# Weights of a gated feed-forward layer loaded and cast by GpSimd's queue at the start of the kernel

## The chip, the cores and the metric

One core of a Trainium2 chip runs the whole program. The metric is the device time of one execution in microseconds (us); lower is better. The profile is of one execution, taken by the hardware profiler; its span is the time from its first to its last recorded event.

## What is computed

Attention with decay over blocks of 64 positions, for 4 batches, 8 heads, 768 positions and a head size of 64, and then a gated ("highway") layer over the 3072 x 512 result:

```python
intra = np.einsum('bhic,bhjc->bhij', qb, kb) * Dmask[None]
intra = np.einsum('bhij,bhjd->bhid', intra, vb)
inter = np.einsum('bhid,bhde->bhie', qb * lam_pow[None], kv_state)
out[:, :, sl] = intra + inter
kv_state = lam_block * kv_state + np.einsum('bhsd,bhse->bhde', kb_dec, vb)
...
H = np.maximum(x @ w_h, 0.0)
T = 1.0 / (1.0 + np.exp(-(x @ w_t + b_t)))
return T * H + (1.0 - T) * x
```

q, k, v, the two 512 x 512 weights `w_h` and `w_t`, the bias and the output are float32.

## The kernel before

The kernel works on 12 chunks n of 256 positions, three to a batch. A chunk has two halves b of 128 positions. A name such as q0 or k1 means q of chunk 0, k of chunk 1. Nothing is scheduled by the machine: the string `PLAN` (L17 to L68) is a list of steps in the order in which they are written to the engines' queues, and every engine works through its own steps in that order. A step is a letter, the chunk and its parts, the engine behind @ and the PSUM banks behind =. The steps that matter here:

- `Lq`, `Lk`, `Lv` (function `load`, L214): loads of q, k and v, in f32, two of 256 KB for each chunk and tensor, all issued by SyncE (SP). There are five buffers of each kind (`BUFS`, L70), so the first five chunks' loads wait for nothing but their turn. One row in DRAM is 1 KB long for q (four positions of 64 floats) and 512 B for k and v.
- `CK`, `CQ`, `CV` (L230, L235, L242): casts of k, q and v to bf16, q and v with a multiplication by powers of lambda.
- `TK`, `TQ` (L255): transposes of k and q on TensorE; `EB` (L268) copies the result to SBUF as `kqT`.
- `S`, `SP`, `U`, `I`, `A` (L291 to L364): the matmuls of the scores, of the state, and of the output of the attention; `M` (L343) multiplies the scores with the mask `tri`, `KE` copies the state, `D` (L366) copies the output to SBUF as `xT`.
- `F` (L389): the matmuls of the feed-forward layer, x times w_h or w_t, with the bf16 weights `w_b`. `PB`, `G`, `H`, `X`, `AD`, `ST` are the bias, the sigmoid, the gating, the sum and the store.
- `W` (`load_w`, L223) and `WC` (`cast_w`, L227): loads and casts of the weights. SP issues four loads of 512 KB, `W.0.0`, `W.0.1`, `W.1.0`, `W.1.1` (weight, half of its rows), to the f32 buffers `w_f`; their rows in DRAM are 2 KB long. Eight casts of 128 x 512 copy them to `w_b`: five on ScalarE (ACT), two on VectorE (DVE), one on GpSimd (POOL). The first step that needs them is `F.0.0.0`.
- `Z` (`spin`, L421) and `ZT`: matmuls on a blank tile whose results are not used, which fill TensorE's waits, above all in the first 17 us.

Ahead of the plan stands the set-up (L123 to L169): ACT loads lambda and the bias and a table, POOL makes the identity, two lists of indices (iota, L135 and L137) and the mask `tri` (L139 to L142), and DVE and ACT make the powers of lambda. A copy or cast on ACT or DVE has the line of the helper `copy` (L110, L112); on POOL L112 too.

Of the kernel before, what the change touches and what calls it, by code (L numbers as in the profile page):

```python
# [16 lines left out]
PLAN = """  # L17
Lq.0.1 Lq.0.0 CQ.0.1@POOL CQ.0.0@POOL Lk.0.0 Lk.0.1 CK.0.0@DVE ZT Z.6=6 TQ.0.0=01 Lv.0.0 Lv.0.1 CK.0.1@ACT Lq.1.0
Lq.1.1 TK.0.0 EB.0.0@ACT EB.0.1@DVE Z.5=6 S.0.0=01 CV.0.1@DVE CV.0.0@DVE Z.3=6 U.0.0 B=2 Lk.1.0 Lk.1.1 Lv.1.0
KE.0.0@DVE CQ.1.0@POOL I.0.1=3 S.0.1=45 U.0.1 CK.1.1@POOL Lv.1.1 PT@ACT M.0.1.1@DVE CK.1.0@DVE M.0.0.1@DVE CQ.1.1@POOL  # L20
CV.1.0@POOL Lq.2.1 Lk.2.0 Lk.2.1 Lq.2.0 W.0.0 Z.5=6 TK.1.1=56 TQ.1.1 M.0.0.0@DVE EB.1.1@DVE CV.1.1@POOL M.0.1.0@DVE
EB.1.0@ACT W.0.1 KE.0.1@ACT BC@ACT Z.7=4 SP.1.0=561 KE.1.0@ACT M.1.1.1@DVE M.1.1.0@DVE Lv.2.1 Lv.2.0 A.0.1=2 A.0.0
I.1.1=0 I.1.0=4 SP.1.1=6 CK.2.2@POOL D.0.1@ACT D.0.0@ACT M.1.0.0@DVE M.1.0.1@DVE W.1.0 TK.2.1=35 W.1.1 KE.1.1@ACT
WC.0.0.1@ACT WC.0.0.0@DVE Lq.3.1 Lq.3.0 WC.0.1.1@DVE WC.0.1.0@ACT CQ.2.2@POOL XT.0=2 A.1.1 A.1.0 D.1.1@DVE TQ.2.1
D.1.0@ACT F.0.0.0=6 XE.0@DVE EB.2.0@ACT XT.1=0 F.1.1.0=2 CV.2.2@POOL WC.1.1.0@POOL EB.2.1@DVE XE.1@DVE PB.0.1@ACT=4
WC.1.0.1@ACT PB.0.0@ACT=1 H.1.1@DVE WC.1.0.0@ACT F.0.1.0=5 F.1.0.0=0 H.0.0@DVE SP.2.0=362 H.0.1@DVE H.1.0@DVE Lk.3.0
Lk.3.1 M.2.1.1@DVE M.2.1.0@DVE M.2.0.0@DVE WC.1.1.1@ACT F.0.1.1 KE.2.0@ACT PB.1.1@ACT=0 G.0.1@ACT F.0.0.1 I.2.1=3
I.2.0=6 X.0.1@DVE SP.2.1=2 F.1.1.1 M.2.0.1@DVE CQ.3.2@POOL Lv.3.0 PB.1.0@ACT=5 AD.0.1@POOL TQ.3.0=24 Lv.3.1 G.0.0@ACT
CK.3.2@ACT Lq.4.0 Lq.4.1 TK.3.0 CV.3.2@POOL CQ.4.2@POOL X.0.0@DVE A.2.1 A.2.0 EB.3.1@ACT EB.3.0@DVE D.2.1@DVE
G.1.1@ACT D.2.0@ACT F.1.0.1 X.1.1@DVE SP.3.0=426 G.1.0@ACT KE.3.0@ACT Lk.4.0 Lk.4.1 Lv.4.0 XT.2=0 Lv.4.1 I.3.1=3  # L30
M.3.0.0@DVE M.3.1.1@DVE AD.1.1@POOL XE.2@ACT CK.4.2@ACT SP.3.1=1 F.2.1.0=6 M.3.0.1@DVE CV.4.2@POOL TQ.4.0=02 Lk.5.0
# [44 lines left out]
def kernel(  # L76
# [30 lines left out]

    def copy(eng, dst, src):
        if eng == "ACT":
            A.activation(dst, src, AF.Copy)  # L110
        else:
            ENG[eng].tensor_copy(dst, src)  # L112
# [26 lines left out]
    P.memset(tri, 1.0)  # L139
# [37 lines left out]
    made = {}

    def new(key, shape, dtype=BF16, tag=None):
        if key not in made:  # L180
            tag = tag or key[0]
            i = turn_of.get(tag, 0)
            turn_of[tag] = (i + 1) % BUFS[tag]
            if (tag, i) not in kept:
                kept[tag, i] = singles.tile(shape, dtype, name=f"{tag}{i}")
            made[key] = kept[tag, i]
        return made[key]
# [20 lines left out]
    def heads(p):  # L208
        return slice(0, H) if p == 2 else slice(4 * p, 4 * p + 4)


    SRC = {"k": k, "q": q, "v": v}

    def load(x, n, p, eng):  # L214
        b, c = divmod(n, NST)
        hs = heads(p)
        src = SRC[x][b, hs, c * 2 * C:(c + 1) * 2 * C, :]
        if x == "q":
            nc.sync.dma_start(out=new((x + "f", n), [128, 4, 4 * D], F32)[p::2], in_=src.rearrange("h (g i) d -> g h (i d)", i=4))  # L219
        else:  # L220
            nc.sync.dma_start(out=new((x + "f", n), [128, H, J * D], F32)[:, hs], in_=src.rearrange("h (p j) d -> p h (j d)", j=J))

    def load_w(w, g):  # L223
        nc.sync.dma_start(out=w_f[w][:, 2 * g:2 * g + 2, :],
# [163 lines left out]

    def block(n, b, w, p=None, bk=()):  # L389
        cs = cols(p)  # L390
        t = get("t", n, b)[:, cs] if w else bank(("h", n, b, p), bk[0], [C, cs.stop - cs.start])
        for kc in range(KC):
            T.matmul(t, lhsT=get("xT", n, b)[:, kc, :], rhs=w_b[w][:, kc, cs],  # L393
                     start=(w == 0 and kc == 0), stop=(kc == KC - 1), skip_group_check=bool(w))
# [30 lines left out]
    def open_banks():  # L425
        for t in banks:
            T.matmul(t, lhsT=id128, rhs=blank, start=True, stop=True)
# [53 lines left out]
```

## Time and profile before

| | |
|---|---|
| three runs | 105.46, 105.39, 101.47 us (median 105.39) |
| the profiled execution | 102.49 us, span 100.3 us |
| busy, share of the span | TensorE (PE) 91%, VectorE (DVE) 81%, GpSimd (POOL) 74%, ScalarE (ACT) 72% |
| transfers | 28.60 MB, mean 285 GB/s |
| loads of q, k, v | 24 each, 256 KB each, 5.0 to 5.5 us from issue to landing |
| loads of the weights | 4, 512 KB each, 6.2 and 7.8 us from issue to landing |

Rows of the chain of work give start, length and the engine with its line. Rows of the waits give who waited for what: us in total, times, and the longest. A tile's view gives the shortest, median and longest duration in ns and the first and last start. In the table of stretches, each engine's busy time with the number of its instructions in brackets is followed by TensorE's granted clock, the mean share of the 16 transfer engines that was busy (over 1 where packets overlap), and GB/s. In the order of time, the bracket at the end of a row is the engine's idle time before it and what ended it. PEld is TensorE's weight load; a q behind an engine's name is its issuing part. "mean" and "busy" of TensorE overlap, since matmuls are pipelined.

### The profile page before, as it was taken

Reading aid. Unit: us, or ns where it says so; the run is one execution under the profiler, and the core shown is the slowest. Engines: PE = TensorE matmul, PEld = TensorE weight load, DVE = VectorE, ACT = ScalarE, POOL = GpSimd, SP = SyncE. Lnnn points to the kernel's source line nnn. Section 1 sums busy time; section 2 is a strip of 40 time slices with the busy share of each in tenths; the row PEclk is TensorE's granted clock in tenths of the full one; section 3 lists DMA queues with packets and bytes.
Section 4 is the critical chain, followed back from the end, with each engine's and each line's share of the span. In section 5 each row is a group of like instructions: output and inputs, shape, how many; then the busy total and the mean of one; then the engine's idle time right before and its main releaser. Section 6 shows DMA issues by size and latency. Waiting matters only on the chain.

```text
span 100.3 us, 4427 instructions
## 1 busy us (share of the span) xinstructions
PE 91.0 (91%) x1891; PEld 54.3 (54%) x1891; DVE 80.8 (81%) x143; ACT 72.2 (72%) x123; POOL 74.2 (74%) x64
## 2 busy tenths in 40 slices
PE   4967999999998999999999899999999999999710
PEld 1314465965454675657665567467466456447500
DVE  4304568899997799999998978999997996896890
ACT  2406507887888899999979997896999968392410
POOL 6180498934679998999989989999984889029640
PEclk9999999999999999999999999999999999999995
DMA  0899999999989999999988999999999972586973
GB/s 6 240 263 323 324 351 374 376 396 371 324 284 325 315 326 331 328 308 288 309 266 250 313 296 285 362 367 337 276 255 358 231 178 97 105 330 158 405 256 109
DMA packets 41221, 28.60 MB, mean 285 GB/s; under 512 B 6129, under 2 KB 37361, under 8 KB 41202
## 3 DMA queue, kind: packets, MB, share of 16 engines
q1 hardware_dynamic: 41056, 28.32, 91.8%
q8 instruction: 14, 0.23, 0.9%
q14 instruction: 5, 0.04, 0.1%
q10 hardware_dynamic: 146, 0.01, 0.1%
HBM read 20.98 MB, written 6.29 MB: 272 GB/s over the span
## 4 chain that ended last, share of the span: by engine, by line
PE 75%; DVE 7%; ACT 6%; DMA 5%; SPq 2%; issue 1%; ACTq 0%; DVEq 0%
PE pb L393 40%; PE pb L291 8%; PE pb L362 5%; DMA kf<-in_k_dram 5%; DVE m L344 5%; PE pb L423 5%; PE pb L352 5%; PE pb L266 4%; PE kv L296 3%; PE pb L263 2%; PE pb L374 2%; ACT kqT L110 2%; ACT pb L406 2%; SPq L219 1%; DVE gxh L409 1%
## 5 line engine op out<-in xcount | busy, mean ns | idle before, releaser
L393 PE MATMUL pb<-w_b,xT 128*128 128x512 bf16 (+1 forms) x208 | 46.6, 364 | 0.5 <-ACT pb L406 0.4
L344 DVE TENSOR_TENSOR m<-pb,tri 128x512 bf16<-128x512 f32 x48 | 31.0, 683 | 4.3 <-PE pb L291 2.7
L412 POOL TENSOR_TENSOR o<-gx,xr 128x512 f32<-128x512 bf16 x22 | 25.2, 1155 | 8.9 <-DVE gx L409 6.5
L238 POOL TENSOR_TENSOR qb<-qf,pow_q 128x1024 bf16<-128x1024 f32 (+1 forms) x14 | 23.2, 1657 | 7.3 <-DMA qf<-in_q_dram 6.5
L393 PEld LDWEIGHTS <-xT 128*128 128x128 bf16 x208 | 18.3, 98 | 17.3 <-issue 0.9
L245 POOL TENSOR_TENSOR vs<-vf,pow_v 128x1024 bf16<-128x1024 f32 (+1 forms) x12 | 21.2, 1773 | 2.7 <-DMA vf<-in_v_dram 1.8
L406 ACT ACTIVATE pb<-pb 128x512 f32<-128x512 f32 (+1 forms) x26 | 14.1, 550 | 5.4 <-PE pb L393 4.3
L110 ACT ACTIVATE kqT<-pb 128x1024 bf16<-128x1024 bf16 x12 | 12.2, 1022 | 6.0 <-PE pb L263 4.0
L409 DVE TENSOR_TENSOR gx<-pb,hm 128x512 bf16<-128x512 f32 x22 | 15.0, 684 | 1.1 <-ACT pb L406 0.3
L401 DVE SCALAR_TENSOR_TENSOR hm<-pb,xr 128x512 bf16<-128x512 f32 x22 | 14.7, 685 | 0.9 <-PE pb L393 0.8
L291 PE MATMUL pb<-kqT 64*64 64x128 bf16 x384 | 14.8, 220 | 0.6 <-ACT xT L110 0.3
L387 ACT ACTIVATE pb<-bt_all 128x512 f32<-128x512 f32 x24 | 14.1, 601 | 0.9 <-DVE m L344 0.5
L291 PEld LDWEIGHTS <-kqT 64*64 64x64 bf16 x384 | 11.1, 106 | 3.9 <-ACT kqT L110 1.2
L110 ACT ACTIVATE xT<-pb 128x512 bf16<-128x512 f32 x19 | 10.9, 594 | 2.7 <-PE pb L362 2.6
L110 ACT ACTIVATE kb<-kf 128x1024 bf16<-128x1024 f32 (+1 forms) x10 | 10.1, 1010 | 3.1 <-DMA kf<-in_k_dram 3.1
L296 PE MATMUL kv<-vs,kb 64*64 64x64 bf16 x320 | 12.0, 193 | 0.0
L296 PEld LDWEIGHTS <-kb 64*64 64x64 bf16 x320 | 9.8, 107 | 0.6 <-issue 0.4
L112 DVE COPY kqT<-pb 128x1024 bf16<-128x1024 bf16 x12 | 8.2, 687 | 2.3 <-PE pb L266 2.2
L362 PE MATMUL pb<-m,vs 64*64 64x128 bf16 x384 | 7.9, 219 | 0.6 <-issue 0.3
L362 PEld LDWEIGHTS <-vs 64*64 64x64 bf16 x384 | 6.1, 106 | 3.0 <-issue 2.8
L110 ACT ACTIVATE ss<-kv 128x256 bf16<-128x256 f32 x17 | 6.5, 382 | 1.7 <-PE pb L291 1.0
L423 PE MATMUL pb<-blank,id 128*128 128x512 bf16 x26 | 7.3, 420 | 0.0
(58 smaller groups left out, 82.7 us busy)
## 6 DMA issues: line engine op xcount, KB each, us to landing
qf<-in_q_dram SPq DMA_DIRECT2D x24, 256.0 KB, 5.0
kf<-in_k_dram SPq DMA_DIRECT2D x24, 256.0 KB, 5.2
vf<-in_v_dram SPq DMA_DIRECT2D x24, 256.0 KB, 5.5
out_dram<-o SPq DMA_DIRECT2D x22, 256.0 KB, 3.2
w_f<-in_moe_w_h_dram SPq DMA_DIRECT2D x2, 512.0 KB, 6.2
w_f<-in_moe_w_t_dram SPq DMA_DIRECT2D x2, 512.0 KB, 7.8
out_dram<-oh SPq DMA_DIRECT2D x4, 128.0 KB, 2.2
xr<-xT SPq DMA_TRANSPOSE x8, 2.6
```

Source lines behind the costliest of these rows:

```text
L110: A.activation(dst, src, AF.Copy)
L238: ENG[eng].tensor_tensor(new(("qb", n), [128, 4, 4, D])[:, :, ys], in0=get("qf", n)[:, ys].rearrange("p y (i d) -> p i y d", i=4), in1=pow ...
L245: ENG[eng].tensor_tensor(new(("vs", n), [128, H, J, D])[:, hs], in0=get("vf", n)[:, hs].rearrange("p h (j d) -> p h j d", j=J), in1=pow_v[ ...
L291: T.matmul(get("s", n, e, hp // 2)[half(b), hp % 2, j, :], lhsT=keys(n, e, hp, j, b), rhs=queries(n, e, hp, b), start=first("s", n, e, hp ...
L296: T.matmul(kv[half(e), hp], lhsT=get("kb", n)[half(b), j, 2 * hp + e, :], rhs=get("vs", n)[half(b), 2 * hp + e, j, :], start=fresh, stop=T ...
L344: V.tensor_tensor(new(("m", n, e, u), [128, 2, J, C]), in0=get("s", n, e, u), in1=tri[:, None].to_broadcast([128, 2, J, C]), op=ALU.mult)
L362: T.matmul(get("o", n, b)[half(e), hp, :], lhsT=get("vs", n)[half(b), 2 * hp + e, j, :], rhs=get("m", n, e, u)[half(b), hp % 2, j, :], sta ...
L393: T.matmul(t, lhsT=get("xT", n, b)[:, kc, :], rhs=w_b[w][:, kc, cs], start=(w == 0 and kc == 0), stop=(kc == KC - 1), skip_group_check=boo ...
L401: V.scalar_tensor_tensor(small("hm", n, b, p), in0=get("h", n, b, p), scalar=0.0, in1=get("xr", n)[:, b, cols(p)], op0=ALU.max, op1=ALU.su ...
L406: A.activation(t, t, AF.Sigmoid)
L409: V.tensor_tensor(small("gx", n, b, p), in0=get("t", n, b)[:, cols(p)], in1=get("hm", n, b, p), op=ALU.mult)
L412: ENG[eng].tensor_tensor(small("o", n, b, p, F32), in0=get("gx", n, b, p), in1=get("xr", n)[:, b, cols(p)], op=ALU.add)
```

## The change

The four loads of the weights leave SP and the plan. POOL issues them in the set-up, after its two iotas and before `tri`, with float32 in DRAM as the source and the bfloat16 tiles `w_b` as the destination, so that the transfer itself casts. The buffers `w_f` and all eight casts go; the plan is otherwise the same list in the same order. ACT's table load is now written ahead of its load of the bias. The diff also moves functions up and adds some that the plan doesn't use (loads issued by ACT, a transposition over two banks, another form of the gating), which leave no instruction.

```diff
-CV.1.0@POOL Lq.2.1 Lk.2.0 Lk.2.1 Lq.2.0 W.0.0 Z.5=6 TK.1.1=56 TQ.1.1 M.0.0.0@DVE EB.1.1@DVE CV.1.1@POOL M.0.1.0@DVE
-EB.1.0@ACT W.0.1 KE.0.1@ACT BC@ACT Z.7=4 SP.1.0=561 KE.1.0@ACT M.1.1.1@DVE M.1.1.0@DVE Lv.2.1 Lv.2.0 A.0.1=2 A.0.0
+CV.1.0@POOL Lq.2.1 Lk.2.0 Lk.2.1 Lq.2.0 Z.5=6 TK.1.1=56 TQ.1.1 M.0.0.0@DVE EB.1.1@DVE CV.1.1@POOL M.0.1.0@DVE
...
-    w_f = [singles.tile([128, KC, DM], F32, name=f"w_f{i}") for i in range(2)]
...
     bt_r = singles.tile([1, DM], F32)
...
+    A.preload_act_table_set("natural_log_exp_and_others")
     A.dma_start(out=bt_r, in_=moe_b_t[None, :])
...
     tq_i = singles.tile([128, NST, 4], I32)
     P.iota(tq_i, pattern=[[2 * C, NST], [1, 4]], base=0, channel_multiplier=2)
+    w_b = [singles.tile([128, KC, DM], BF16, name=f"w_b{i}") for i in range(2)]
+    for g in range(2):
+        for w in range(2):
+            P.dma_start(out=w_b[w][:, 2 * g:2 * g + 2, :],
+                        in_=(moe_w_h, moe_w_t)[w][256 * g:256 * g + 256, :].rearrange("(kc p) m -> p kc m", p=128))
     tri = singles.tile([128, J, C], F32)
...
-    A.preload_act_table_set("natural_log_exp_and_others")
...
-    w_b = [singles.tile([128, KC, DM], BF16, name=f"w_b{i}") for i in range(2)]
```

POOL's queue before, from the iotas of the set-up to the casts of the second chunk (`x2` is two such rows in a line):

```order
L135 IOTA tk_i 128x6
L137 IOTA tq_i 128x12
L139 MEMSET tri 128x256
L141 AFFINE_SELECT tri<-tri 64x256 x2
L238 TENSOR_TENSOR qb_156<-qf_69,pow_q 128x4x128 x2
L238 TENSOR_TENSOR qb_265<-qf_70,pow_q 128x4x128
L112 CAST kb_307<-kf_65 128x4x2x64
```

The same place now; the lines have other numbers since functions moved:

```order
L166 IOTA tk_i 128x6
L168 IOTA tq_i 128x12
L172 DMA w_b_114<-in_moe_w_h_dram 128x2x512
L172 DMA w_b_115<-in_moe_w_t_dram 128x2x512
L172 DMA w_b_114<-in_moe_w_h_dram 128x2x512
L172 DMA w_b_115<-in_moe_w_t_dram 128x2x512
L175 MEMSET tri 128x256
L177 AFFINE_SELECT tri<-tri 64x256 x2
L245 TENSOR_TENSOR qb_158<-qf_69,pow_q 128x4x128 x2
```

Four issues stand ahead of the mask and of the first casts of q, which TensorE's first transposes read.

SP's queue before, from the loads of the third chunk (buffers 71, 66, 76 of q, k and v) on:

```order
L219 DMA qf_71<-in_q_dram 64x4x256
L221 DMA kf_66<-in_k_dram 128x4x128 x2
L219 DMA qf_71<-in_q_dram 64x4x256
L224 DMA w_f_95<-in_moe_w_h_dram 128x2x512 x2
L221 DMA vf_76<-in_v_dram 128x4x128 x2
L224 DMA w_f_96<-in_moe_w_t_dram 128x2x512 x2
L219 DMA qf_72<-in_q_dram 64x4x256 x2
```

And now:

```order
L145 DMA qf_71<-in_q_dram 64x4x256
L147 DMA kf_66<-in_k_dram 128x4x128 x2
L145 DMA qf_71<-in_q_dram 64x4x256
L147 DMA vf_76<-in_v_dram 128x4x128 x2
L145 DMA qf_72<-in_q_dram 64x4x256 x2
```

The weights stood between the third chunk's k and v and the fourth chunk's q; now the loads of q, k and v follow each other there. In ACT's queue, where the five casts stood between the first copies of the attention's output and the first sigmoid, the rows around them close up in the same order.

More of the change, by code (lines that the diff above doesn't have):

```diff
@@ L20 @@
 KE.0.0@DVE CQ.1.0@POOL I.0.1=3 S.0.1=45 U.0.1 CK.1.1@POOL Lv.1.1 PT@ACT M.0.1.1@DVE CK.1.0@DVE M.0.0.1@DVE CQ.1.1@POOL
-CV.1.0@POOL Lq.2.1 Lk.2.0 Lk.2.1 Lq.2.0 W.0.0 Z.5=6 TK.1.1=56 TQ.1.1 M.0.0.0@DVE EB.1.1@DVE CV.1.1@POOL M.0.1.0@DVE
-EB.1.0@ACT W.0.1 KE.0.1@ACT BC@ACT Z.7=4 SP.1.0=561 KE.1.0@ACT M.1.1.1@DVE M.1.1.0@DVE Lv.2.1 Lv.2.0 A.0.1=2 A.0.0
[L23 to L28, printed above, removed]
+CV.1.0@POOL Lq.2.1 Lk.2.0 Lk.2.1 Lq.2.0 Z.5=6 TK.1.1=56 TQ.1.1 M.0.0.0@DVE EB.1.1@DVE CV.1.1@POOL M.0.1.0@DVE
+EB.1.0@ACT KE.0.1@ACT BC@ACT Z.7=4 SP.1.0=561 KE.1.0@ACT M.1.1.1@DVE M.1.1.0@DVE Lv.2.1 Lv.2.0 A.0.1=2 A.0.0 I.1.1=0
+I.1.0=4 SP.1.1=6 CK.2.2@POOL D.0.1@ACT D.0.0@ACT M.1.0.0@DVE M.1.0.1@DVE TK.2.1=35 KE.1.1@ACT Lq.3.1 Lq.3.0
+CQ.2.2@POOL XT.0=2 A.1.1 A.1.0 D.1.1@DVE TQ.2.1 D.1.0@ACT F.0.0.0=6 XE.0@DVE EB.2.0@ACT XT.1=0 F.1.1.0=2 CV.2.2@POOL
+EB.2.1@DVE XE.1@DVE PB.0.1@ACT=4 PB.0.0@ACT=1 H.1.1@DVE F.0.1.0=5 F.1.0.0=0 H.0.0@DVE SP.2.0=362 H.0.1@DVE H.1.0@DVE
+Lk.3.0 Lk.3.1 M.2.1.1@DVE M.2.1.0@DVE M.2.0.0@DVE F.0.1.1 KE.2.0@ACT PB.1.1@ACT=0 G.0.1@ACT F.0.0.1 I.2.1=3 I.2.0=6
+X.0.1@DVE SP.2.1=2 F.1.1.1 M.2.0.1@DVE CQ.3.2@POOL Lv.3.0 PB.1.0@ACT=5 AD.0.1@POOL TQ.3.0=24 Lv.3.1 G.0.0@ACT
 CK.3.2@ACT Lq.4.0 Lq.4.1 TK.3.0 CV.3.2@POOL CQ.4.2@POOL X.0.0@DVE A.2.1 A.2.0 EB.3.1@ACT EB.3.0@DVE D.2.1@DVE
@@ L121, with new, heads, load @@
             kept[tag, i] = singles.tile(shape, F32, name=f"{tag}{i}")
-    w_f = [singles.tile([128, KC, DM], F32, name=f"w_f{i}") for i in range(2)]
+    made = {}
+    def new(key, shape, dtype=BF16, tag=None):
+        if key not in made:
+            tag = tag or key[0]
+            i = turn_of.get(tag, 0)
+            turn_of[tag] = (i + 1) % BUFS[tag]
+            if (tag, i) not in kept:
+                kept[tag, i] = singles.tile(shape, dtype, name=f"{tag}{i}")
+            made[key] = kept[tag, i]
+        return made[key]
+    def heads(p):
+        return slice(0, H) if p == 2 else slice(4 * p, 4 * p + 4)
+    SRC = {"k": k, "q": q, "v": v}
+    def load(x, n, p, eng):
+        b, c = divmod(n, NST)
+        hs = heads(p)
+        src = SRC[x][b, hs, c * 2 * C:(c + 1) * 2 * C, :]
+        e = A if eng == "ACT" else nc.sync
+        if x == "q":
+            e.dma_start(out=new((x + "f", n), [128, 4, 4 * D], F32)[p::2], in_=src.rearrange("h (g i) d -> g h (i d)", i=4))
+        else:
+            e.dma_start(out=new((x + "f", n), [128, H, J * D], F32)[:, hs], in_=src.rearrange("h (p j) d -> p h (j d)", j=J))
     lam_all = singles.tile([128, H], F32)
@@ L125 @@
     bt_r = singles.tile([1, DM], F32)
+    early = [x for x in PLAN.split() if x[0] == "L" and x.endswith("@ACT")]
+    for token in early:
+        name, *args = token.partition("@")[0].split(".")
+        load(name[1], int(args[0]), int(args[1]), "ACT")
+    A.preload_act_table_set("natural_log_exp_and_others")
     A.dma_start(out=bt_r, in_=moe_b_t[None, :])
@@ L169 @@
     A.activation(pow_v, p_ln, AF.Exp, scale=-1.0)
-    w_b = [singles.tile([128, KC, DM], BF16, name=f"w_b{i}") for i in range(2)]
     pair = ps.tile([128, 512], F32, name="kv")
     kv = pair[:, 0:256].rearrange("p (n d) -> p n d", d=64)
[L177 to L187, printed above, removed]
     banks = [ps.tile([128, 512], F32, name=f"pb{i}") for i in range(7)]
@@ L206, in get @@
         return made[key]
[L208 to L221, printed above, removed]
     def load_w(w, g):
@@ L370, in turn, with evac_x @@
     def turn(n, bk):
-        t = bank(("x", n), bk[0], [C, 2, KC, 128], BF16)
+        if len(bk) == 1:
+            t = bank(("x", n), bk[0], [C, 2, KC, 128], BF16)
+        else:
+            t = [bank(("x", n, e), bk[e], [C, 2, KC, 64], BF16) for e in range(2)]
         for b in range(2):
             for j in range(KC):
-                T.transpose(t[:, b, j, :], get("xT", n, b)[:, j, :], id128)
-    def evac_x(n, eng):
-        copy(eng, new(("xr", n), [C, 2, DM]), get("x", n).rearrange("p b j f -> p b (j f)"))
+                if len(bk) == 1:
+                    T.transpose(t[:, b, j, :], get("xT", n, b)[:, j, :], id128)
+                else:
+                    for e in range(2):
+                        T.transpose(t[e][:, b, j, :], get("xT", n, b)[half(e), j, :], id128[half(e), half(e)])
+    def evac_x(a, eng):
+        n, xr = a[0], new(("xr", a[0]), [C, 2, DM])
+        if len(a) == 1:
+            copy(eng, xr, get("x", n).rearrange("p b j f -> p b (j f)"))
+        else:
+            copy(eng, xr.rearrange("p b (j e f) -> p e (b j) f", e=2, f=64)[:, a[1]], get("x", *a).rearrange("p b j f -> p (b j) f"))
     def turn_dma(n, b):
@@ L412, in add, with sigm_s, part, rest @@
         ENG[eng].tensor_tensor(small("o", n, b, p, F32), in0=get("gx", n, b, p), in1=get("xr", n)[:, b, cols(p)], op=ALU.add)
+    def sigm_s(n, b, p):
+        A.activation(small("gs", n, b, p, F32), get("t", n, b)[:, cols(p)], AF.Sigmoid)
+    def part(n, b, p, eng):
+        ENG[eng].tensor_tensor(small("gw", n, b, p, F32), in0=get("gs", n, b, p), in1=get("xr", n)[:, b, cols(p)], op=ALU.mult)
+    def rest(n, b, p, eng):
+        ENG[eng].tensor_tensor(small("gv", n, b, p, F32), in0=get("xr", n)[:, b, cols(p)], in1=get("gw", n, b, p), op=ALU.subtract)
+    def gated(n, b, p):
+        V.scalar_tensor_tensor(small("gr", n, b, p, F32), in0=get("h", n, b, p), scalar=0.0, in1=get("gs", n, b, p),
+                               op0=ALU.max, op1=ALU.mult)
+    def total(n, b, p, eng):
+        ENG[eng].tensor_tensor(small("o", n, b, p, F32), in0=get("gr", n, b, p), in1=get("gv", n, b, p), op=ALU.add)
     def store(n, b, p=None):
@@ L437 @@
         "XD": lambda a, e, bk: turn_dma(*a),
-        "XT": lambda a, e, bk: turn(*a, bk), "XE": lambda a, e, bk: evac_x(*a, e), "PB": lambda a, e, bk: preset(*a, bk),
+        "XT": lambda a, e, bk: turn(*a, bk), "XE": lambda a, e, bk: evac_x(a, e), "PB": lambda a, e, bk: preset(*a, bk),
         "F": lambda a, e, bk: block(*a, bk=bk), "H": lambda a, e, bk: relu(*a), "G": lambda a, e, bk: sigm(*a),
@@ L442 @@
         "ZT": lambda a, e, bk: open_banks(),
+        "GS": lambda a, e, bk: sigm_s(*a), "GX": lambda a, e, bk: part(*a, e), "GW": lambda a, e, bk: rest(*a, e),
+        "HR": lambda a, e, bk: gated(*a), "OT": lambda a, e, bk: total(*a, e),
         "PT": lambda a, e, bk: A.preload_act_table(AF.Sigmoid),
@@ L445 @@
     }
-    for token in PLAN.split():
+    for token in [x for x in PLAN.split() if x not in early]:
         token, _, bk = token.partition("=")
```

## Prediction

> **What bounds the kernel now.** I read the busy table first, then the chain of work that ended last, then the waits, then the first 27 us in order of time. The chain, by engine and then by time:
>
> ```profile
> PE 75%; DVE 7%; ACT 6%; DMA 5%; SPq 2%; issue 1%; ACTq 0%; DVEq 0%
> ...
> 2.26 0.60 SPq L221
> 2.90 5.16 DMA kf<-in_k_dram
> 8.08 0.64 ACT kb L110
> 8.76 0.29 PE pb L266 x8
> 9.05 1.19 PE pb L423 x5
> ...
> 15.80 1.51 PE pb L423 x7
> ...
> 17.97 2.48 DVE m L344 x4
> ...
> 22.99 2.59 PE pb L393 x12
> ...
> 30.43 1.02 ACT kqT L110
> ```
>
> Three quarters of the chain is TensorE. The only transfer on it is the first load of k, issued at 2.26 and landed at 8.06. Behind it the chain runs through TensorE in its written order, with filler matmuls (L423) in the gaps. No load or cast of the weights stands anywhere on it. So a microsecond by which the first loads come late moves all that follows, and a microsecond of cast that goes away is not taken off the chain. From 40 to 50 us TensorE is busy for 9.96 of 10, DVE for 9.58, ACT for 9.70, POOL for all 10: no engine has room to make up a late start.
>
> ```profile
> 0.00:5.00 5.00, 3.58 (x9) 1.34 (x10) 2.02 (x11) 1.87 (x4) 2.06 (x11) 1.00 0.43 123
> 20.00:25.00 5.00, 4.75 (x68) 2.94 (x66) 4.73 (x9) 4.08 (x8) 1.90 (x1) 1.00 1.08 384
> 40.00:50.00 10.00, 9.96 (x262) 6.50 (x259) 9.58 (x16) 9.70 (x16) 10.00 (x7) 1.00 1.04 310
> ...
> 3.00:8.00 5.00, 4.11 (x34) 1.58 (x32) 1.26 (x5) 0.66 (x4) 2.05 (x2) 1.00 0.92 276
> 8.00:13.00 5.00, 4.41 (x78) 2.03 (x75) 2.31 (x4) 2.94 (x3) 1.27 (x2) 1.00 1.05 325
> 17.00:19.00 2.00, 2.00 (x111) 1.62 (x111) 1.18 (x3) 1.14 (x4) 2.00 (x2) 1.00 1.05 397
> ```
>
> The columns behind the busy times are TensorE's granted clock, the DMA share and GB/s. From 3 us on the transfer engines are full, at 0.92 and then 1.05 of their time. The kernel's opening is a queue of transfers, and the waits say the same: POOL, ACT and DVE stand still there for q, k and v.
>
> ```profile
> POOL qb L238 <- DMA qf<-in_q_dram: 6.3, 2, 3.6
> ACT kb L110 <- DMA kf<-in_k_dram: 3.1, 1, 3.1
> DVE kb L112 <- DMA kf<-in_k_dram: 2.7, 1, 2.7
> POOL vs L245 <- DMA vf<-in_v_dram: 1.8, 1, 1.8
> ```
>
> **What the change removes.** Eight casts and four issues:
>
> ```profile
> L110 ACT ACTIVATE w_b<-w_f x5: 614/631/642, 19.7 to 25.3; 128x512 bf16<-128x512 f32 x5
> L224 SPq DMA_DIRECT2D w_f<-in_moe_w_h_dram x2: 467/537/607, 13.2 to 13.9; - x2
> L224 SPq DMA_DIRECT2D w_f<-in_moe_w_t_dram x2: 468/570/672, 16.2 to 16.9; - x2
> L112 DVE CAST w_b<-w_f x2: 420/422/423, 20.3 to 20.7; 128x512 bf16<-128x512 f32 x2
> L112 POOL CAST w_b<-w_f x1: 609/609/609, 25.0 to 25.0; 128x512 bf16<-128x512 f32 x1
> ...
> 26.18 0.39 ACT L110 ACTIVATE ss<-kv 128x256 bf16<-128x256 f32 x1 [0.25 <-PE pb L291]
> ```
>
> That is 5 x 0.63 = 3.1 us of ACT, 0.8 of DVE, 0.6 of POOL and 4 x 0.55 = 2.2 of SP. I take nothing for it. While the casts run, from 19.7 to 25.9, the chain is on DVE's masks up to 20.4 and then on TensorE; right behind the last of them ACT waits 0.25 us for TensorE (last row). An ACT that is done earlier waits longer. The bounds are 0 and, if all of ACT's time there stood on the path, 3.1 us of gain. SP's 2.2 us are worth nothing while the transfer engines are full: SP only fills their queue earlier. The cover for that is the DMA share of 1.08 in 20 to 25 us; without it, later loads would come up to 2.2 us earlier, and none of them is on the chain.
>
> The table load that ACT now starts before the issue of the bias instead of after it is free either way: what it precedes waits for lam until 3.60. The bias row is first used at 11.64. Both rows:
>
> ```profile
> 3.60 0.21 ACT L155 ACTIVATE ln_all<-lam_all 128x8 f32<-128x8 f32 x1 [0.52 <-DMA lam_all<-in_lam_dram]
> 11.64 1.12 PE L419 MATMUL pb<-bt_r,ones 1*128 1x512 f32 x2
> ```
>
> **What it adds on POOL.** Four issues between the iota that starts at 1.43 and the mask `tri`:
>
> ```profile
> 1.52 0.31 POOL L139 MEMSET tri<- 128x256 f32 x1
> 1.91 0.94 POOL L141 TENSOR_SCALAR_AFFINE_SELECT tri<-tri 64x256 f32<-64x256 f32 x2
> 5.49 2.05 POOL L238 TENSOR_TENSOR qb<-qf,pow_q 128x512 bf16<-128x512 f32 x2 [2.65 <-DMA qf<-in_q_dram]
> 12.77 0.61 POOL L112 CAST kb<-kf 128x512 bf16<-128x512 f32 x1 [0.55 <-DMA kf<-in_k_dram]
> 13.34 1.05 POOL L238 TENSOR_TENSOR qb<-qf,pow_q 128x512 bf16<-128x512 f32 x1
> 14.35 2.22 POOL L245 TENSOR_TENSOR vs<-vf,pow_v 128x512 bf16<-128x512 f32 x2
> ```
>
> No row shows what an issue costs on POOL. From below, SP's for the same shape: 0.55, so 2.2 in all, inside the 2.65 us that POOL waits for q before 5.49. From above, the longest kind of work that POOL does here, 1.9 us for 128x1024 (median of the page's q casts), so 7.6. I take 1.0, nearer to SP's row because it is the same transfer: 4.0, so `tri` ends at 2.85 + 4.0 = 6.85 and the first cast of q starts 1.4 us late. Queued behind it on POOL are the casts of q that TensorE's first transposes wait for. But q and k come late as well (next term), k by more than 1.4, so this is hidden up to about 5.85/4 = 1.5 us per issue (2.65 of waiting and 3.2 of k's lateness, 5.85); past that POOL is the bound, and that is a rival below.
>
> [...]
>
> **What it adds on the transfer engines.** Four transfers of 512 KB are 2.10 MB. They used to be issued from 13.21 on, behind the first two chunks' q, k and v and the third's q and k (q0 to v1, q2, k2); now they start at about 2.6 to 6 us and share the engines with q0 to v1. At the 397 GB/s of 17 to 19 us, when weights were in flight, they take 5.3 us of engine time (6.5 at the 325 of 8 to 13 us; their rows in DRAM are four times as long as those of k and v, so I take the first). Some room is there: 3 to 8 us moved 276 GB/s where 8 to 13 moved 325, a lack of 0.25 MB or 0.7 us. So a load that the weights have wholly passed comes 5.3 - 0.7 = 4.6 us late.
>
> *Path through k1 and v1.* k1 lands at 12.77 and v1 by 14.35 now. By then the weights have nearly all passed, so +4.6. From k1's landing POOL casts k (12.77), then q (ends 14.39); TensorE's transposes of that q start at 15.19:
>
> ```profile
> 15.19 0.61 PE L263 MATMUL pb<-id,qb 128*128 128x128 bf16 x8
> ```
>
> That is 0.8 us of slack: 4.6 - 0.8 = +3.8 at the transposes, and all the later chain follows.
>
> *Path through k0.* At 3.6 us about 0.2 of the 1.05 MB of q0 and k0 has moved (0.615 MB by 5 us, from the first stretch's 123 GB/s, less 1.4 us at 276). If the two queues share evenly, the other 0.85 MB at half of 325 takes 5.2 us instead of 3.1 at 276: +2.1. If they alternate row by row, where the code's rows are 2 KB for the weights, 1 KB for q and 512 B for k, then q gets a third of 397 GB/s up to 5.9 us and k a fifth while the weights last, up to 10.6; k0 is complete near 11.05 instead of 6.7: +4.3. I take 3.2, the middle, since no row shows two busy queues.
>
> TensorE then stands idle from 6.70 until about 8.76 + 3.2 = 12.0, apart from the transposes of q. Its filler shows what a start from rest costs:
>
> ```profile
> L423 PE MATMUL pb<-blank,id x14: 379/384/634, 4.4 to 11.0; 128*128 128x512 bf16 x14
> L427 PE MATMUL pb<-blank,id x7: 606/634/635, 1.4 to 4.0; 128*128 128x512 bf16 x7
> ...
> 1.43 3.17 PE L427 MATMUL pb<-blank,id 128*128 128x512 bf16 x7 [1.43 <-POOL id masks.py:199]
> ```
>
> The first seven took 634 ns and came (3.17 - 0.63)/6 = 0.42 us apart; those from 9.05 on 1.19/5 = 0.24. If the array is slow again after the longer gap, the ten 512-column matmuls that now run between 9 and 12.8 cost 10 x 0.18 = 1.8 us more. Half of that falls into waits that exist anyway: I take 0.9, from bounds of 0 and 1.8. So +3.2 + 0.9 = +4.1 on this path.
>
> [...]
>
> **Sum.** The paths join at the second chunk's scores near 17 us, so the later one counts, not both: +4.1. The profiled execution took 102.49 us with a span of 100.3: 102.49 + 4.1 - 0 = **106.6 us**. From the low ends (k1's path with 0.7 more slack at its next steps, some ACT time back) to the high ends (k0 row by row and slow filler, 6.1) the forecast's own range is 104.3 to 108.6. The median shown, 105.39, lies 2.9 above the profiled execution (the lowest is 101.47); the same 4.1 on it gives 109.5, and the range's upper end covers that.
>
> **Rivals.**
>
> *The weights do not hold up the loads.* A second queue may get only what the first leaves, or start late. For it: the weights are not needed until 21.5, and 3 to 5 us has some room. Against it: a share of 0.92 to 1.05 means that what one queue gets the other lacks. Then the casts' 3.1 us were not on the chain either, and the time is 102.49 less a few tenths: 102.2. It decides if k0 still lands by 8.5. [...] No row here has two busy queues.
>
> *POOL becomes the bound.* At 1.9 us per issue `tri` ends at 10.4, the first q cast starts 4.9 late, and slow filler adds up to 1.8: 102.49 + 6.7 = 109.2. It decides from 1.5 us per issue. Against it: SP's 0.55.
>
> *Faster: ACT was the hidden bound of 19.7 to 26.* If the loads are not held up and ACT's order, not TensorE, set the pace there, its 3.1 us come off: 99.4. For it: ACT is busy 4.08 of 5 us in 20 to 25, with sigmoids and state copies queued behind the casts. Against it: the wait of 0.25 for TensorE right after them, and a chain without them. It decides if ACT's wait before 26.18 does not grow.
>
> **How the numbers follow.** Loads late: 0.57 (106.6). POOL as bound: 0.09 (109.2). Loads not held up: 0.21 (102.2). ACT as bound: 0.13 (99.4). About 2% (2.1 us) is what a measurement of this kernel can tell from no change. Slower by more: the first two, less 0.01 for a small delay: 0.65. Faster: the last and 0.03 of the third: 0.16. Within: 0.19. The range of 101.4 to 109.6 leaves out most of the ACT case, and beyond the POOL case only its worse half.
>
> **What would show it.** Right: the first k lands near 11.3 instead of 8.06; TensorE idles from about 7 to 12 but for q's transposes; the transposes of the second chunk's q start near 19 instead of 15.19; the chunks' work from there on keeps its lengths; ACT has the five casts less and waits longer. Wrong: k0 landing before 9, or the steps after 17 us catching up by more than a microsecond until 40, or four POOL issues of over 1.5 us each.

## The result and the profile after

| | before | after |
|---|---|---|
| runs beside each other | 101.47, 101.95, 105.39, 105.46 us (median 103.67) | 108.67, 109.10, 109.53, 115.10 us (median 109.31) |
| the profiled execution | 102.49, span 100.3 | 108.67, span 107.0 |
| busy: PE, DVE, ACT, POOL (us) | 91.0, 80.8, 72.2, 74.2 | 92.9, 80.3, 69.5, 76.6 |

After over before is 1.067, 95% interval 1.060 to 1.074: slower by 6 to 7.5 us. Some executions of every version take a few per cent longer throughout; the ratios leave these out, and where a ratio and a median differ below, I go by the ratio.

From the page of the changed kernel: the chain by engine, the granted clock in 40 slices, and the two queues that matter (packets, MB, share of 16 engines).

```profile
PE 61%; DVE 14%; DMA 9%; ACT 9%; issue 2%; SPq 2%; DVEq 0%; ACTq 0%
PEclk9998558999999999999999999999999999999997
q0 software_dynamic: 1088, 1.05, 6.1%
q1 hardware_dynamic: 39968, 26.22, 81.0%
```

The transfers' part of the chain has grown from 5% to 9%, the clock has a hole in the fourth to the seventh slice (8 to 18.7 us, at 0.5 in the middle two), and POOL's queue (q0) is new. Its 1.05 MB are the bytes written, in bf16; twice as many are read.

The chain of the changed kernel in order of time (start, length, what):

```profile
2.90 9.82 DMA kf<-in_k_dram
12.75 0.64 ACT kb L109
13.44 0.39 PE pb L273 x6
13.83 2.25 PE pb L457 x5
...
17.86 1.05 PE pb L453 x2
...
20.31 0.80 DVE kb L111
21.15 1.07 PE pb L270 x16
22.22 1.51 PE pb L457 x7
24.39 2.48 DVE m L351 x4
29.41 2.59 PE pb L411 x12
...
36.85 1.02 ACT kqT L109
```

Row by row against before: k0's cast starts at 12.75 instead of 8.08, **+4.7**. The five fillers behind k0's transposes take 2.25 instead of 1.19; the bias matmuls start at 17.86 instead of 11.71, +6.2, so **1.5** more were lost on TensorE: 1.06 in these five fillers, the rest in the transposes and scores beside them. Then DVE's cast of k1, which was not on the chain before, stands on it (the trace has it at 0.87 us, 0.59 before), and the second chunk's transposes run at 21.15 instead of 14.78, +6.4. From there to the copy at 36.85 (before 30.43, +6.4) every length is the old one: 1.51, 2.48, 2.59. All the loss lies before 21 us.

The waits for the first loads (us in total, times, longest), and the stretches (busy time of PE, PEld, DVE, ACT, POOL, then granted clock, DMA share, GB/s):

```profile
POOL qb L245 <- DMA qf<-in_q_dram: 8.6, 1, 8.6
ACT kb L109 <- DMA kf<-in_k_dram: 7.7, 1, 7.7
```

```profile
3.00:8.00 5.00, 3.93 (x10) 1.21 (x8) 0.78 (x4) 0.58 (x3) 4.79 (x8) 1.00 1.05 225
8.00:13.00 5.00, 0.80 (x24) 0.52 (x24) 0.43 (x1) 0.25 (x1) 0.11 (x1) 0.70 1.19 225
...
40.00:50.00 10.00, 9.77 (x270) 6.12 (x268) 9.39 (x17) 9.05 (x14) 9.64 (x8) 1.00 1.08 323
```

From 8 to 13 us TensorE works 0.80 of 5 us, where it worked 4.41, while the transfer engines are full (a share of 1.19; the GB/s count what is written, 1.05 MB on q0 for 2.10 MB read, so they are low while the weights are read in f32 and written in bf16). ACT's wait for k0 has grown from 3.1 to 7.7 us.

What POOL does in the opening, and what ACT does with the time that the casts left it, from the order of time:

```profile
1.57 0.89 POOL L172 DMA_DIRECT2D w_b<-in_moe_w_h_dram  x1
2.45 0.74 POOL L172 DMA_DIRECT2D w_b<-in_moe_w_t_dram  x1
...
5.03 0.95 POOL L177 TENSOR_SCALAR_AFFINE_SELECT tri<-tri 64x256 f32<-64x256 f32 x2
6.06 2.05 POOL L245 TENSOR_TENSOR qb<-qf,pow_q 128x512 bf16<-128x512 f32 x2
...
32.61 0.39 ACT L109 ACTIVATE ss<-kv 128x256 bf16<-128x256 f32 x1 [2.50 <-PE pb L298]
```

An issue on POOL takes 0.72 to 0.89 us; `tri` ends at 5.98, and q's first cast starts 0.6 late, long before k0 is there. The last row is the state copy that in the profile before waited 0.25 us for TensorE behind the casts: it now waits 2.50. Most of the 3.1 us that the five casts took on ACT went into this wait.

Which row of the weights got in front of which row of k is in the transfers' view of 8 to 10 us:

```profile
q0 software_dynamic: 294, 0.28, 84.0%
q1 hardware_dynamic: 298, 0.15, 35.6%
```

The same number of packets on both queues: as many rows of the weights (0.28 MB in 294 packets, 0.95 KB each: a row of 2 KB read, written in bf16) as rows of k (0.15 MB in 298, 0.5 KB each: a row of 512 B). 298 x 512 B in 2 us are 76 GB/s for SP's queue, out of 294 x 2 KB + 298 x 512 B = 0.75 MB, or 377 GB/s: a fifth.

The equal count holds from 8 to 12 us (294 and 297 packets in 10 to 12). From 6 to 8 us, k0 has nearly three rows for one of the weights:

```profile
q0 software_dynamic: 192, 0.18, 60.3%
q1 hardware_dynamic: 551, 0.28, 51.2%
```

So from 6 to 12 us k0 has about a quarter of the bytes read (1146 rows of 512 B, 0.59 MB, beside 780 rows of 2 KB, 1.60 MB). What sets the ratio of the rows is not shown.

### The profile page after: what moved, and what is told of

It is laid out like the page before. It is cut to its first block, busy times and chain, and to the rows that moved or that the text cites. A ratio compares the mean times of both kernels' runs of the same rounds, so it can differ in the third digit from the quotient of the medians.

```text
span 107.0 us, 4421 instructions
## 1 busy us (share of the span) xinstructions
PE 92.9 (87%) x1891; PEld 54.7 (51%) x1891; DVE 80.3 (75%) x141; ACT 69.5 (65%) x118; POOL 76.6 (72%) x67
## 3 DMA queue, kind: packets, MB, share of 16 engines
q0 software_dynamic: 1088, 1.05, 6.1%
## 4 chain that ended last, share of the span: by engine, by line
PE 61%; DVE 14%; DMA 9%; ACT 9%; issue 2%; SPq 2%; DVEq 0%; ACTq 0%
PE pb L411 33%; DMA kf<-in_k_dram 9%; DVE m L351 8%; PE pb L298 6%; PE pb L457 4%; PE pb L369 4%; PE pb L273 4%; PE pb L359 3%; ACT kb L109 2%; ACT xT L109 2%; ACT kqT L109 2%; PE kv L303 2%; DVE gx L427 2%; PE pb L385 2%; PE pb L270 2%
## 5 line engine op out<-in xcount | busy, mean ns | idle before, releaser
L427 DVE TENSOR_TENSOR gx<-pb,hm 128x512 bf16<-128x512 f32 x22 | 14.9, 683 | 1.0 <-ACT pb L424 0.3
L457 PE MATMUL pb<-blank,id 128*128 128x512 bf16 x26 | 8.7, 481 | 0.0
L273 PE MATMUL pb<-id,kb 64*128 64x64 bf16 x144 | 4.0, 196 | 4.5 <-ACT kb L109 3.0
```

The costliest lines, as they stand in the source:

```text
L427: V.tensor_tensor(small("gx", n, b, p), in0=get("t", n, b)[:, cols(p)], in1=get("hm", n, b, p), op=ALU.mult)
```

## The experiments

Two groups of kernels ran on one chip, a third on another, each group beside runs of the kernel before (medians 103.95, 103.36 and 103.80 us). Two chunk times recur below: when k0's cast on ACT starts, and how long it is from the first chunk's copy `kqT` on ACT to the second's. Before: 8.08 and 6.30 (9.09 to 15.39). After: 12.75 and 7.94 (13.87 to 21.81).

**e1_late: the same transfers, later.** The four casting transfers stay on POOL's queue, but as steps of the plan (`WP`, issued at 12.5, 14.9, 17.9 and 19.6 us); the casts stay away.

```diff
-    for g in range(2):
-        for w in range(2):
-            P.dma_start(out=w_b[w][:, 2 * g:2 * g + 2, :],
-                        in_=(moe_w_h, moe_w_t)[w][256 * g:256 * g + 256, :].rearrange("(kc p) m -> p kc m", p=128))
...
-KE.0.0@DVE CQ.1.0@POOL I.0.1=3 S.0.1=45 U.0.1 CK.1.1@POOL Lv.1.1 PT@ACT M.0.1.1@DVE CK.1.0@DVE M.0.0.1@DVE CQ.1.1@POOL
+KE.0.0@DVE CQ.1.0@POOL WP.0.0 I.0.1=3 S.0.1=45 U.0.1 CK.1.1@POOL Lv.1.1 PT@ACT M.0.1.1@DVE CK.1.0@DVE M.0.0.1@DVE CQ.1.1@POOL
-CV.1.0@POOL Lq.2.1 Lk.2.0 Lk.2.1 Lq.2.0 Z.5=6 TK.1.1=56 TQ.1.1 M.0.0.0@DVE EB.1.1@DVE CV.1.1@POOL M.0.1.0@DVE
+WP.0.1 CV.1.0@POOL Lq.2.1 Lk.2.0 Lk.2.1 Lq.2.0 Z.5=6 TK.1.1=56 TQ.1.1 M.0.0.0@DVE EB.1.1@DVE CV.1.1@POOL WP.1.0 M.0.1.0@DVE
...
```

> The changed kernel with the four casting transfers issued by GpSimd one at a time between its casts of the second and third chunk (from about 12, 14.5, 17 and 18 us on) instead of ahead of the mask; the casts and f32 buffers stay away. Theory (only the place in front of the first loads costs; the eight casts were never on the path): the first k lands at 8.1 again, the tensor array does not fall back to its slow clock, and the time is within 1 us of before, 101.5 to 103. Rival 1 (a transfer that casts, issued by GpSimd, is slow or disturbs wherever it stands): 104 or more. Rival 2 (ACT's five casts were a hidden bound): 100 or less.

Measured: 103.19, 103.62 and 103.76 us in the three shortest of six runs, 104.82 at the median of the six; before beside it took 101.07 at the lowest and 103.95 at the median. So it lies 0.9 us over before by the medians and 2.1 by the lowest, where the change lies 6 to 7.5 over. By time alone this decides nothing: the three shortest lie between the theory's 101.5 to 103 and the first rival's 104 or more, and the median in the rival's. From the profile (of an execution of 105.87 us), k0's cast on ACT, the stretch of 8 to 13 us, and DVE's cast of k1:

```profile
8.51 0.63 ACT L109 ACTIVATE kb<-kf 128x512 bf16<-128x512 f32 x1 [3.56 <-DMA kf<-in_k_dram]
```

```profile
8.00:13.00 5.00, 3.80 (x55) 1.66 (x48) 1.89 (x3) 2.94 (x3) 1.51 (x2) 0.66 1.06 326
```

```profile
15.84 1.21 DVE L111 CAST kb<-kf 128x512 bf16<-128x512 f32 x1
```

k0 is back at 8.51, and most of the loss is gone: what cost most was the place in time, since these are the same transfers, on the same queue and with the same cast in them. That nothing is left of it is not shown. Against the expectation, this execution has a granted clock of 0.66 in 8 to 13 us with k0 on time, and DVE's cast of k1 takes 1.21 us instead of 0.59; its second chunk's transposes start at 17.11 instead of 14.78. In the three shortest runs the mean granted clock is 0.99, as in the shortest of before, so that fall of the clock is not in them. Whether a gain from the casts and a price of the queue cancel here, the next kernel tells.

**e6_no_casts: the casts alone.** The kernel before without its eight casts. Its bf16 weights are set to zero once, so the feed-forward products are left out of what it computes; the loads stay where they were.

```diff
-WC.0.0.1@ACT WC.0.0.0@DVE Lq.3.1 Lq.3.0 WC.0.1.1@DVE WC.0.1.0@ACT CQ.2.2@POOL XT.0=2 A.1.1 A.1.0 D.1.1@DVE TQ.2.1
+Lq.3.1 Lq.3.0 CQ.2.2@POOL XT.0=2 A.1.1 A.1.0 D.1.1@DVE TQ.2.1
...
+    V.memset(w_b[0], 0.0)
+    V.memset(w_b[1], 0.0)
```

> The kernel before without its eight casts of the weights: the loads by SP stay where they are, the bf16 weights are set to zero once by VectorE in the set-up, so the feed-forward layer's products are left out of the result. Theory (the casts are off the chain): within 0.6 us of before. Rival (ACT's 3.1 us of casts bound the stretch of 19 to 26 us): 1.5 to 3 us faster.

Measured: 102.96 us at the lowest and 103.42 at the median, beside 101.07 and 103.95. The casts are worth half a microsecond by the medians and nothing by the lowest. Neither this kernel nor e1_late has casts, and e1_late is 0.2 us (lowest) to 1.4 us (median) above it: so much can late transfers on POOL's queue cost beside SP's plain ones.

**e2_warm: TensorE kept busy through the longer wait.** The changed kernel with fillers between q's and k's transposes.

```diff
-Lq.0.1 Lq.0.0 CQ.0.1@POOL CQ.0.0@POOL Lk.0.0 Lk.0.1 CK.0.0@DVE ZT Z.6=6 TQ.0.0=01 Lv.0.0 Lv.0.1 CK.0.1@ACT Lq.1.0
+Lq.0.1 Lq.0.0 CQ.0.1@POOL CQ.0.0@POOL Lk.0.0 Lk.0.1 CK.0.0@DVE ZT Z.6=6 TQ.0.0=01 Z.8=6 Lv.0.0 Lv.0.1 CK.0.1@ACT Lq.1.0
...
+                if (n, x, i) == (0, 0, 3):
+                    spin(9, [6])
```

> The changed kernel with 17 more filler matmuls in the gap of the tensor engine, 8 after the first transposes of q and 9 between the two halves of the first transposes of k. Theory (of the 6.4 us, 1.4 are the slow clock between 10 and 17 us): k still lands at 12.7, but the five fillers behind its transposes take 1.2 us instead of 2.25 and the scores 0.35 instead of 0.57; 107.2 to 107.6 against the change's 108.7. Rival (the second chunk's q and k, which land at 16.8 and 18.2, hold the chain next): no more than 0.4 us come off, 108.3 or more.

**e8_warm_again and e7_after_again: the same kernel once more, beside the changed kernel itself,** since e2's opening and its total time said different things.

> The changed kernel as it is, beside the next three on one chip. Theory: k lands near 12.7, slow clock from 10 to 17 us, 6 to 7.5% over before as measured first. Rival (the first measurement's chip made part of it): under 5%.

> The changed kernel with 17 more fillers again, now beside the changed kernel itself on one chip. In the first try the second chunk's scores began 1.8 us earlier than in the change (21.9 against 23.7), but a DMA transpose near the end landed 1.6 us later, so the span did not shrink. Theory (the slow clock costs 1.4 to 1.8 at the start, and the late transpose was one execution's): 1 to 2 us less than the change beside it. Rival (an earlier start is lost again at the end, whatever the cause): within 0.6 us of the change.

Measured: e2 111.24 us median (lowest 109.44); e7 110.81, ratio to before 1.070 (1.060 to 1.080); e8 111.55, ratio 1.076 (1.063 to 1.089). So no gain. In the opening the fillers do what they should: from the first `kqT` to the second it is 6.8 us in e2 and 7.0 in e8, against 7.9 in the changed kernel's first profile and 8.9 in e7's. (In e8 k0 itself was cast 1.1 us later than in e7, at 14.01, so its second `kqT` is only 0.9 us earlier, at 22.02.) Both then lose time near the end, at the same place. The row of e8 (in the first profile of the changed kernel this wait is 0.83 us):

```profile
100.81 0.42 DVE L421 SCALAR_TENSOR_TENSOR hmh<-pb,xr 128x256 bf16<-128x256 f32 x1 [2.44 <-DMA xr<-xT]
```

The last transposing transfer comes 1.6 us later. Why is open. The pages of e2 and e8 count 15 instruction transfers where the changed kernel has 14, and both kernels have more TensorE instructions; but e5 below counts 15 too and waits only 0.8 there. So from the first `kqT` to the second the fillers take off 1 to 2 us, and that this can be won back in the whole is not shown.

**e3_act_f32: no cast, no GpSimd.** The kernel before, its f32 loads of the weights issued by ACT in the set-up; the casts stay.

```diff
+    for g in range(2):
+        for w in range(2):
+            A.dma_start(out=w_f[w][:, 2 * g:2 * g + 2, :],
+                        in_=(moe_w_h, moe_w_t)[w][256 * g:256 * g + 256, :].rearrange("(kc p) m -> p kc m", p=128))
...
-        nc.sync.dma_start(out=w_f[w][:, 2 * g:2 * g + 2, :],
...
```

> The kernel before with its four plain f32 loads of the weights issued by ACT's queue in the set-up, at 1.8 to 4 us, instead of by SP at 13 to 17; no cast in a transfer, nothing by GpSimd, the eight casts as before. ACT's set-up comes about 2.2 us later, which q's late landing should hide. Theory (2.1 MB in rows of 2 KB on any second queue take four fifths of the engines from k's rows of 512 B): the first k lands at 12 to 13.5 and the time is 107.5 to 110. Rival (the cost belongs to GpSimd's queue or to the cast): k lands before 10.5 and the time is below 105.5.

Measured: 109.75 us median, lowest 108.80; k0's cast at 11.72, a little before the 12 to 13.5 expected. Transfers from 8 to 10 us, and one of ACT's issues:

```profile
q10 hardware_dynamic: 313, 0.60, 77.5%
q1 hardware_dynamic: 356, 0.18, 29.5%
```

```profile
6.88 0.42 ACTq L129
```

Almost the same count of packets on two hardware queues, with no cast in a transfer and no transfer issued by GpSimd: here the sharing is no matter of either. (Here too it is not the same throughout: from 6 to 8 us the counts are 237 and 492, from 10 to 12 us 207 and 708.) The test of the total time is partly confounded, because ACT, which also has to make the powers of lambda, is held up by its own issues until 7.3 us.

**e4_rows1k: shorter rows.** Each of the four transfers is made as two of half the columns, so its rows in DRAM are 1 KB.

```diff
-            P.dma_start(out=w_b[w][:, 2 * g:2 * g + 2, :],
-                        in_=(moe_w_h, moe_w_t)[w][256 * g:256 * g + 256, :].rearrange("(kc p) m -> p kc m", p=128))
+            for c in range(2):
+                P.dma_start(out=w_b[w][:, 2 * g:2 * g + 2, 256 * c:256 * c + 256],
+                            in_=(moe_w_h, moe_w_t)[w][256 * g:256 * g + 256, 256 * c:256 * c + 256].rearrange("(kc p) m -> p kc m", p=128))
```

> The changed kernel with each of the four early transfers cut into two of 256 columns: rows of 1 KB instead of 2 KB in DRAM, the same 2.1 MB, eight issues on GpSimd, about 6 us instead of 3. Theory (the two queues alternate row by row, so the bytes go by the rows' lengths): while weights are in flight k gets a third instead of a fifth of the bytes; the first k lands 1 to 2.5 us earlier than the 12.7 of the change, the weights last longer, the first cast of q starts near 9; 1 to 2.5 us less than the change. Rival (the queues share evenly by bytes or by time): k lands within 0.5 us of 12.7 and the time is the same or, for the longer issue, more.

Measured: 111.82 us median beside e7's 110.81: the expected time was missed. k0's cast is 1.35 us earlier than in e7 (11.53 against 12.88), as the sharing by rows said. Transfers from 12 to 14 us, and what waited for them:

```profile
q0 software_dynamic: 410, 0.20, 72.2%
q1 hardware_dynamic: 416, 0.26, 56.4%
```

```profile
16.39 1.29 DVE L253 TENSOR_TENSOR vs<-vf,pow_v 128x512 bf16<-128x512 f32 x2 [3.02 <-DMA vf<-in_v_dram]
```

Still about row for row; but the weights, with the same bytes to move, now last longer (361 packets still in 14 to 16 us, none there in the changed kernel), and v0 pays: DVE waits 3.02 us for it until 16.39, where it waited 0.75 until 15.34 in the changed kernel. What k0 gained here, v0 lost.

**e5_one_early: one transfer of the four at the start.** `WP.0.0` in the set-up, the other three late as in e1.

```diff
-    for g in range(2):
-        for w in range(2):
-            P.dma_start(out=w_b[w][:, 2 * g:2 * g + 2, :],
-                        in_=(moe_w_h, moe_w_t)[w][256 * g:256 * g + 256, :].rearrange("(kc p) m -> p kc m", p=128))
+    P.dma_start(out=w_b[0][:, 0:2, :], in_=moe_w_h[0:256, :].rearrange("(kc p) m -> p kc m", p=128))
```

> Only the first of the four casting transfers (0.52 MB) stays ahead of the mask; the other three are issued by GpSimd after its casts of the second chunk's q and v and the third's k, as in the run with all four late. [...] Rival (a fixed cost of using the second queue early): 4 us or more over before.

Measured: ratio to before 1.013 (1.003 to 1.023), or 1.3 us, with k0's cast at 8.66 (8.08 before, 12.75 after the change). A quarter of the early bytes has about a fifth of the price; a fixed cost of early issues on POOL, the rival, would have left most of it. In the profile (of an execution of 109.85 us) the granted clock is 0.66 in 8 to 13 us, though k0 is on time; I had not expected that.

**e10_cold: a slow TensorE without late loads.** The kernel before without the six fillers that run from 4.4 us.

```diff
-Lq.0.1 Lq.0.0 CQ.0.1@POOL CQ.0.0@POOL Lk.0.0 Lk.0.1 CK.0.0@DVE ZT Z.6=6 TQ.0.0=01 Lv.0.0 Lv.0.1 CK.0.1@ACT Lq.1.0
+Lq.0.1 Lq.0.0 CQ.0.1@POOL CQ.0.0@POOL Lk.0.0 Lk.0.1 CK.0.0@DVE ZT TQ.0.0=01 Lv.0.0 Lv.0.1 CK.0.1@ACT Lq.1.0
```

> The kernel before, its weights loaded by SP in their old place, with one thing taken out: the six filler matmuls that TensorE runs at about 4.4 us, while it waits for the first q and k. They compute nothing that is used. The loads are those of before, so the first k should land at 8.1 to 8.9 us as there. Theory (the slow clock is a cost of its own, apart from late loads): TensorE stands still from about 4.6 us to 8.7 but for q's transposes, its granted clock falls to 0.50 in the records around 8 to 12 us, the five fillers behind k's transposes take about 0.43 us each instead of 0.24, and the time from the cast of k to the second chunk's transposed k (before 22.35 us, after the change 24.2) grows by 1.3 to 2.0: 1 to 2 us over the kernel before in its time. Rival (the clock costs nothing by itself, what the change costs is all in the late loads): no more than 0.5 us over it, and the clock either stays at 1.00 or its fall moves nothing.

Measured: 105.16 us median, ratio 1.026 (1.012 to 1.040). k0's cast is even earlier (7.33). Its granted clock and two rows of the fillers, the first to be compared with 1.19 for five, and the transposes of the second chunk, 1.02 before and 1.07 after:

```profile
PEclk9999999999999999999999999999999999999999
```

```profile
8.61 2.25 PE pb L423 x5
...
17.14 1.91 PE pb L423 x4
19.06 1.61 PE pb L263 x16
```

In this profile TensorE is slow from 8.6 to about 20 us, with loads that come on time, and the kernel without the six fillers is 1.3 to 4 us slower. (The profiled execution took 107.68 us; how long the spell lasts in the shorter ones is not seen. From the first `kqT` to the second it has 11.3 us instead of 6.3, and 1.05 of that is DVE's cast of k1, at 1.64 instead of 0.59.) The rival, at most 0.5 us, falls; the theory, that a slow TensorE has a price without late loads, holds, with a price at or above the 1 to 2 us expected. The expected sign was wrong: the granted clock stays at 1.00 throughout, and the slowness shows only in the distances between matmuls. And the cause may differ from that in the changed kernel: here the array has only its first seven matmuls behind it when it comes to rest, 0.42 us apart (3.17 us for all), and the five at 8.61 come 0.45 apart; whether it was fast in between is not shown.

**e9_q0_act: a candidate.** e1_late, with the two issues of q0 moved to ACT, so that SP's first issue is that of k0.

```diff
-Lq.0.1 Lq.0.0 CQ.0.1@POOL CQ.0.0@POOL Lk.0.0 Lk.0.1 CK.0.0@DVE ZT Z.6=6 TQ.0.0=01 Lv.0.0 Lv.0.1 CK.0.1@ACT Lq.1.0
+Lq.0.1@ACT Lq.0.0@ACT CQ.0.1@POOL CQ.0.0@POOL Lk.0.0 Lk.0.1 CK.0.0@DVE ZT Z.6=6 TQ.0.0=01 Lv.0.0 Lv.0.1 CK.0.1@ACT Lq.1.0
```

> The kernel with the weights' casting transfers on GpSimd's queue late (those of e1_late, 12 to 20 us), and the two issues of the first q moved from SP to ACT, ahead of its table load, so that SP's first issue is that of k. A candidate to be faster than both kernels: k's issue is then at about 1.1 instead of 2.26 us. Theory (the opening is bound by the transfers' bytes, not by issues: share 0.92 and over from 3 us on): k can be up to 1.1 us earlier only at q's expense; expected k's cast at 7.4 to 8.5 us, the chain up to 1 us shorter, and the time 0 to 1 us below e1_late's 103.5, so within 1% of the kernel before. Rival (ACT's issues and table load get in the way of its cast of k, as in e3_act_f32): k's cast no earlier, and a time equal to e1_late's or up to 1 us over it.

Measured: 108.96 us median, ratio 1.061 (1.047 to 1.075): as slow as the change, with the first issue of the weights only at 11.59 us. Both expectations missed, though k0's cast did move, to 7.11. Transfers from 4 to 6 us, and what POOL waits for:

```profile
q1 hardware_dynamic: 727, 0.36, 60.4%
q10 hardware_dynamic: 241, 0.23, 37.0%
```

```profile
8.59 2.05 POOL L245 TENSOR_TENSOR qb<-qf,pow_q 128x512 bf16<-128x512 f32 x2 [5.74 <-DMA qf<-in_q_dram]
```

In the kernel before, with all of these on SP's queue, q0 was cast at 5.49. Here k and v run beside q0 (727 packets against 241 from 4 to 6 us), which is cast at 8.59; TensorE rests longer (no matmul from 6 to 10 us) and starts slowly (granted clock 0.50 in 12 to 14 us), and the second chunk is 5.5 us late. The packets here go three to one, as in the changed kernel from 6 to 8 us, so the equal count is not a rule for two queues; why was not tried. No version that I ran beats the kernel before.

## Why the prediction was wrong

The direction and the mechanism were right: the loss comes from loads that are late in the opening, and of the two paths the one through k0 counts. The size was not. From one profiled execution to the other the forecast was +4.1 us and the measured difference is +6.2 (102.49 to 108.67); that the median, 109.31, still lies in the range is owed to its upper end, which was drawn for a base of 105.39. What failed is the size of two terms.

- **"I take 3.2, the middle, since no row shows two busy queues."** This is the step that failed most. I had worked out both sharings, +2.1 if even and +4.3 if row by row, and took the mean of the two. The runs showed something close to the row by row one: 294 against 298 packets and a fifth of the bytes for k from 8 to 12 us, though more before, 551 rows against 192 from 6 to 8; and k0 came 4.7 late. The 0.4 over the upper end has at least two parts, of opposite sign. The rate was lower than the 397 GB/s assumed: by the same working the two queues together read 320 GB/s from 4 to 6 us, 338 from 6 to 8 and 377 from 8 to 12. And k0 had more than its fifth from 6 to 8. How much each part is worth was not measured. (The working also has k0 of before complete at 6.7 us, where it landed at 8.06; only the difference went into the sum.)
- **"Half of that falls into waits that exist anyway: I take 0.9."** It was 1.5, and nothing of it fell into waits, as the chain in order of time before already showed: between 8.76 and 17.97 nearly all of it is TensorE. Nor did it come as counted, 0.18 for each of ten matmuls. The first five cost 1.06 more and the transposes and scores beside them 0.3; the other three fillers cost 0.1 and the two bias matmuls nothing (1.05 in both kernels), since the slow spell was over by then (granted clock 0.80 in 16 to 18 us and 1.00 in 18 to 20). Those five took 2.25 us at a granted clock of 0.50 (12 to 16 us), and 1.19 before at 1.00.
- **Path through k1:** k1 was cast on POOL at 18.19 instead of 12.77, +5.4 for a predicted 4.6. With the 0.8 of slack it would have given +4.6 at the transposes, and it is the smaller one, as the prediction had it. The DVE cast of k1, 0.3 longer, was not foreseen.
- **POOL's issues:** 0.72 to 0.89 us for an estimate of 1.0, hidden as said. **The casts at nothing:** right (e6_no_casts, and ACT's wait of 2.50).
- **The rivals:** loads not held up falls with k0's wait of 7.7 us, ACT as hidden bound with its longer wait. POOL as bound had 109.2, by chance nearly the time measured, but for a reason that the rows rule out: its condition was 1.5 us per issue.
- **"Later work keeps its lengths":** right; +6.4 at 21 us, +6.4 at 37 and 6.7 in the span.

The sum with what was measured: 4.7 + 1.5 + 0.3 = 6.5, and 102.49 + 6.5 = 109.0, against 108.67 of the profiled execution.

That the slow spell and the late loads are separate prices is shown for the opening: by e10_cold (a slow TensorE with k0 on time) and by e2_warm and e8_warm_again (late loads with TensorE kept busy, 1 to 2 us less from the first `kqT` to the second). The spell also came in profiles of e1_late and e5_one_early with k0 on time (granted clock 0.66 in 8 to 13 us in both), so late loads are not its only occasion; what sets it off there is open. DVE's cast of k1 stands behind both prices and took 0.58 to 2.59 us; what stretches it was not tested.

## What to carry to other kernels

In this kernel the opening is a queue of transfers in the order of their need, and a second queue busy beside it broke that order: with three kinds of load (one that casts, a plain one, and q0 itself) it cost about 6 us or more. Here a bulk load of 2 KB rows left the 512 B rows that the chain waits for a quarter of the bytes, at times a fifth. If two mechanisms give two prices and no row tells them apart, give each its own time and chance; the middle between them is a price that neither gives. A load that is needed only later was better issued when the first ones had landed (e1_late: the same transfers, 1 to 2 us over before instead of 6 to 7.5).
